# Moving element-wise work to GpSimd and the first weights to the head of the queue

## The chip, the cores and the metric

The kernel runs on one core of one Trainium2 chip. The core has five engines that work side by side, each through its own instructions strictly in their order: TensorE (PE in the rows; PEld is its loading of weights), VectorE (DVE), ScalarE (ACT), GpSimd (POOL) and SyncE (SP, which here issues most of the DMAs). The metric is the device time of the core in microseconds (us), from one launch.

## The reference

The inputs pass three stages. For B = 4 batch items, H = 8 heads, S = 576 rows and D = 64 columns:

```
a     = softmax(causal(q k^T / sqrt(D)))                 # scores
local = a v
q_p   = phi(q) = max(q, 0) + exp(min(q, 0))              # elu(q) + 1
mem   = (q_p M_prev) / (q_p . z_prev + 1e-6)
attn  = g mem + (1 - g) local,  g = sigmoid(beta) by head
x = attn as 2304 rows x 512
x = (s * relu(x w_in)^2 + b) w_out        # 512 -> 2048 -> 512
x = h * tanh(softplus(h)) w_out2, h = x w_in2             # mish, 512 -> 2048 -> 512
```

The weights of both feed-forward layers arrive as 64-bit floats.

## The kernel before

**Attention.** 64 zero rows are put ahead of the queries, so that 640 rows make five row tiles of 128, t = 0 to 4. The unit of work is a *pair*: two heads of one batch item, for one group of row tiles. Group TA is the tiles 0 to 2, group TB the tiles 3 and 4; 16 of each make 32 pairs, here numbered 0 to 31 in the order in which they are worked on. Pairs 0 to 3 are the TA pairs of the first batch item; from pair 4 on TB pairs (even numbers) and TA pairs (odd numbers) take turns. For each pair and head a tile `Pt` of 128 rows has 64 columns for the memory part in front, and behind them the scores of row tile t, 64 + 128 t columns. The steps, with the lines of the profile:

1. L494 (GpSimd) min(q, 0) for the whole pair, 384 columns for TA and 256 for TB; L495 (ScalarE) its exponential; L496, L497, L498 (VectorE) phi(q), times z, and the row sums; L492 and L500 gate and reciprocal of these, `nm`.
2. L526 (TensorE) scores into PSUM; L532 (VectorE) adds the mask, takes the row minimum and copies into `Pt`; L543 (GpSimd) writes the memory part; L540 (ScalarE) the exponential with row sums `rs`.
3. L561 (VectorE) reciprocal of the gated `rs`; L558 scales the scores of each row tile by it, in place, one instruction for each tile and head. Which engine does it is in the string `E_NORM`, by t: GpSimd for t = 0, 1, 2 and VectorE for t = 3, 4.
4. L581 (TensorE) turns `Pt` by blocks of 128, in two groups for a head of a TA pair and three for one of a TB pair; L586 copies each group from PSUM to `PT`. `E_TURN` says on which engine, by head and group: all on ScalarE but the first group of the second head of TA pairs (384 columns), which is VectorE's.
5. L603 (TensorE) the product with [M; v]; L617 (ScalarE) copies it out. For pairs 0 to 3 L614 and L615 make the first 256 rows of layer 1's input from it at once.

**Weights.** Each of the 32 pieces (128 x 512) of layer 1's weights, four for each of eight weight tiles (`w_in` and `w_out`, r = 0 to 3), is made from 64-bit words by `convert`: an SP load of 512 KB (L653); the high words times 2^-112 (L660, 512 elements, every second 4-byte word, on ScalarE by `C_W`); the low words (L665, ScalarE); sign and merge (L667, L669, VectorE); a rounded high part (L676, ScalarE) and the rest (L679, VectorE). Layer 2's pieces do the same by `C2_W`, into another place.

**Layer 1** (L762 in, L838 out, with L811, L817, L820, L822 between) works on blocks of 256 rows, later 512. Its first matmul needs the outputs of pairs 0 to 3 and the first weights. Layer 2 (L968, L1034) follows.

**What sets the order.** Nothing is issued as it is written. `Plan` collects steps with an engine, a duration (`act_us`, `dve_us`, `pool_us` or a number in the call), a priority and what they wait for, runs a list scheduler over them, and writes the program in the order found. Attention pairs have priority 7 x their number, layer 1's matmuls 500 and more, so that TensorE takes attention work first and fills what is left with layer 1. Before the first matmul of layer 1 it fills idle time with products of zeros (L1215). A number in a call thus moves instructions on every engine.

Of the kernel before, what the change touches and what calls it, by code (L numbers as in the profile page):

```python
# [9 lines left out]
F32 = mybir.dt.float32  # L10
# [5 lines left out]
ALU = mybir.AluOpType  # L16
# [7 lines left out]
PE, ACT, DVE, POOL, DMA = range(5)  # L24
# [8 lines left out]

E_NORM = 'PPPDD'
E_TURN = {0: 'AAAAA', 1: 'DAAAA'}
C_HI, C_W, C2_W = 'AAAA', 'AAAA', 'AAAA'
C_LO = 'DDDD'
# [16 lines left out]
def pool_us(n):  # L54
    return 0.2 + 0.0033 * n

# [5 lines left out]
def on(letter):  # L62
    return {"A": ACT, "D": DVE, "P": POOL}[letter]
# [266 lines left out]
def attention_then_two_ffn(ctx: ExitStack, tc: tile.TileContext, qk, qz, vm, beta,  # L330
# [3 lines left out]
    nc = tc.nc  # L334
# [97 lines left out]
    def pair(b, p, prio, g, place=None, apart=False):  # L432
# [4 lines left out]
        def add(engine, us, f, r=(), w=(), keep=(), share=1.0):  # L437
            attention_steps.append(plan.add(engine, us, prio, f, r, w, keep=keep, share=share))
# [30 lines left out]
        def q_rows():  # L469
            return part(qn_b, 1, n_t + 1)[:, :, 1:]  # L470
# [22 lines left out]

        add(POOL, 0.3 + 0.0032 * n_e, lambda: nc.gpsimd.tensor_scalar_min(ex.t, q_rows(), 0.0), [qn_b], [ex])  # L494
        add(ACT, act_us(n_e), lambda: nc.scalar.activation(ex.t, ex.t, AF.Exp), [ex], [ex])  # L495
# [66 lines left out]
        for t in g:  # L562
            for i in range(2):
                e = on(E_NORM[t])
                n = D + P * t
                us = act_us(n) if e == ACT else 0.05 + dve_us(n, True) if e == DVE else pool_us(n)
                add(e, us, lambda i=i, t=t, e=e: scale(i, t, e), [done, Pt_in[i, t]], [Pt_in[i, t]], [Pt[i, t][0], rs])
# [71 lines left out]
    def convert(layer, prio, which, r, j, raw, after=()):  # L639
# [7 lines left out]
        def words():  # L647
            return raw.t[:, :1024].rearrange("p (n two) -> p n two", two=2)

        def f32():  # L650
            return w.t.bitcast(F32)
# [6 lines left out]
        e = on((C_W if layer == 1 else C2_W)[j])  # L658
        add(e, 0.52 if e == ACT else 0.335, prio,
            (lambda: nc.scalar.activation(f32(), words()[:, :, 1].bitcast(F32), AF.Copy, scale=2.0 ** -112)) if e == ACT else  # L660
            (lambda: nc.vector.tensor_scalar(f32(), words()[:, :, 1].bitcast(F32), 2.0 ** -112, None, op0=ALU.mult)),
            [raw], [w])
# [438 lines left out]
    for i, p in enumerate(pieces):  # L1101
        convert(1, 3.0 * i if i < 8 else 28.0 + 3.0 * (i - 8), *p, raws[i])
    conversion_left = add(NONE, 0.0, 0.0, lambda: None, after=plan.steps[n:])
# [160 lines left out]
```

## Time and profile before

| | us |
|---|---|
| median of 3 runs | 996.66 (992.43 to 996.84) |
| profiled execution | 996.01 |
| its span, first to last instruction | 994.2 |
| TensorE busy | 972.1 (98%) |
| VectorE busy | 680.9 (68%) |
| ScalarE busy | 635.5 (64%) |
| GpSimd busy | 183.2 (18%) |

The page divides the span in 40 slices of 24.9 us. TensorE's digit is 9 in nearly all of them, but these shares are means over stages with different limits: in the first twelve slices, but for the very first, VectorE and ScalarE stand at 7 to 9 too and GpSimd at 3 to 8. The last output of attention (L617) is copied near 338 us, in slice 14; from then on GpSimd does no arithmetic, and VectorE and ScalarE reach 9 in single slices alone. So the stretches are read one by one, by windows.

### The profile page before, as it was taken

The numbers are of one execution on the slowest core, as the hardware profiler recorded it, in microseconds if no ns is written. First come the engines' busy times: TensorE is split into PE (matmuls) and PEld (weight loads), VectorE is DVE, ScalarE is ACT, GpSimd is POOL, SyncE is SP. The second block draws the span as 40 slices with busy tenths as digits, with TensorE's granted clock in tenths as the row PEclk, the third lists the DMA queues.
The fourth block names the chain that finished last, engine by engine and source line by source line (L and its number), as shares of the span: only waits on it lengthen the run. The fifth ranks groups of instructions, "written<-read, shape, count | busy, mean of one in ns | idle before, by whom it ended". The sixth has DMA issues, their size and how long they took to land.

```text
span 994.2 us, 18129 instructions
## 1 busy us (share of the span) xinstructions
PE 972.1 (98%) x6342; PEld 854.8 (86%) x6342; DVE 680.9 (68%) x1638; ACT 635.5 (64%) x1361; POOL 183.2 (18%) x346
## 2 busy tenths in 40 slices
PE   6999989999999999999999999999999999999998
PEld 4767767877787898888888888999999999999998
DVE  5989889877775467778412143489965799567864
ACT  5988888777775567899645566366643466434552
POOL 5863443465531000000000000000010001100100
PEclk9999999999999999999999999999999999999999
DMA  9962565654441389997700116288677666676465
GB/s 259 300 185 65 172 198 152 168 135 130 127 129 55 94 264 294 297 324 250 260 3 1 43 64 221 96 294 273 212 268 240 202 209 211 237 248 203 150 221 175
DMA packets 103083, 184.69 MB, mean 186 GB/s; under 512 B 17232, under 2 KB 77648, under 8 KB 95696
## 3 DMA queue, kind: packets, MB, share of 16 engines
q1 hardware_dynamic: 95504, 132.15, 43.0%
q0 software_dynamic: 7056, 51.38, 15.2%
q8 instruction: 50, 0.82, 0.3%
q14 instruction: 41, 0.34, 0.1%
q10 hardware_dynamic: 432, 0.01, 0.0%
HBM read 141.04 MB, written 42.47 MB: 185 GB/s over the span
## 4 chain that ended last, share of the span: by engine, by line
PE 79%; issue 7%; DMA 6%; ACT 4%; POOL 2%; DVE 1%; POOLq 0%; SPq 0%; ACTq 0%
PE bank L762 18%; PE bank L838 17%; PE bank L968 15%; PE bank L1034 13%; PE bank L581 5%; PE bank L526 5%; PE bank L603 5%; POOL Pt L558 2%; DMA wo_split_d<-high 1%; DMA woh<-wo_split_d 1%; ACT Pt L540 1%; DMA wol<-wi_split_d 1%; DMA wih<-in_w_in 1%; ACT stage L660 1%; DMA stage<-in_w_in 1%
## 5 line engine op out<-in xcount | busy, mean ns | idle before, releaser
L1034 PE MATMUL bank<-woh,S 128*128 128x256 f32 x792 | 107.4, 283 | 1.4 <-DMA woh<-wo_split_d 1.4
L540 ACT ACTIVATE Pt<-Pt,mx 128x64 f32<-128x64 f32 (+4 forms) x160 | 89.0, 563 | 22.2 <-DVE mx L532 22.0
L1034 PEld LDWEIGHTS bank<-woh,S 128*128 128x128 f32 x792 | 100.8, 192 | 1.6 <-ACT S L690 1.6
L1034 PE MATMUL bank<-wol,S 128*128 128x256 f32 x720 | 98.1, 283 | 0.0
L968 PE MATMUL bank<-wi,woh 128*128 128x384 f32 x426 | 93.9, 334 | 0.0
L949 POOL DMA_DIRECT2D wol<-wo_split_d x17 | 9.2, 541 | 457.4 <-DVE wi L691 365.6
L1034 PEld LDWEIGHTS bank<-wol,S 128*128 128x128 f32 x720 | 91.8, 192 | 0.0
L586 ACT COPY PT<-bank 128x384 f32<-128x384 f32 (+1 forms) x144 | 62.9, 490 | 31.2 <-PE bank L581 28.7
L543 POOL TENSOR_SCALAR Pt<-ex,nm 128x64 f32<-128x64 f32 x160 | 61.6, 404 | 112.4 <-DVE nm L500 54.1
L581 PE MATMUL bank<-ident,Pt 128*128 128x128 f32 x480 | 73.1, 284 | 9.0 <-POOL Pt L558 6.8
L532 DVE CUSTOM_DVE_ANT_0 Pt<-bank,mask 128x320 f32<-128x320 f32 (+3 forms) x160 | 64.0, 430 | 22.6 <-PE bank L526 21.6
L968 PE MATMUL bank<-wi,wol 128*128 128x384 f32 x294 | 76.0, 335 | 0.4 <-DMA wol<-wi_split_d 0.4
L968 PEld LDWEIGHTS bank<-wi,woh 128*128 128x128 f32 x426 | 75.6, 188 | 0.6
L581 PEld LDWEIGHTS bank<-ident,Pt 128*128 128x128 f32 x480 | 55.7, 145 | 17.5 <-POOL Pt L558 10.4
L558 POOL TENSOR_SCALAR Pt<-Pt,rs 128x64 f32<-128x64 f32 (+2 forms) x96 | 60.5, 650 | 40.0 <-DVE rs L561 33.1
L838 PE MATMUL bank<-xh,woh 128*128 128x512 f32 x240 | 64.2, 389 | 0.0
L821 DVE TENSOR_TENSOR xh<-g,xh 128x512 fp32r<-128x512 f32 x30 | 20.6, 688 | 60.2 <-ACT xh L819 60.2
L968 PEld LDWEIGHTS bank<-wi,wol 128*128 128x128 f32 x294 | 53.0, 188 | 0.9 <-DMA wol<-wi_split_d 0.6
L838 PEld LDWEIGHTS bank<-xh,woh 128*128 128x128 f32 x240 | 45.0, 188 | 9.1
L762 PE MATMUL bank<-yh,wi 128*128 128x512 f32 x192 | 51.4, 391 | 0.4 <-ACT g L811 0.4
L811 ACT ACTIVATE g<-bank 128x512 f32<-128x512 f32 x48 | 28.6, 595 | 33.4 <-PE bank L762 33.4
L762 PEld LDWEIGHTS bank<-yh,wi 128*128 128x128 f32 x192 | 35.3, 188 | 7.6 <-ACT g L811 0.8
(256 smaller groups left out, 2335.2 us busy)
## 6 DMA issues: line engine op xcount, KB each, us to landing
wol<-wo_split_d POOLq DMA_DIRECT2D x17, 1024.0 KB, 5.2
woh<-wo_split_d POOLq DMA_DIRECT2D x16, 1024.0 KB, 5.4
stage<-in_w_out SPq DMA_DIRECT2D x23, 512.0 KB, 5.0
wo_split_d<-high SPq DMA_DIRECT2D x44, 256.0 KB, 4.3
stage<-in_w_in SPq DMA_DIRECT2D x21, 512.0 KB, 5.4
stage<-wi_d SPq DMA_DIRECT2D x24, 384.0 KB, 4.8
wi_split_d<-woh SPq DMA_DIRECT2D x8, 1024.0 KB, 4.9
wol<-wi_split_d POOLq DMA_DIRECT2D x8, 1024.0 KB, 5.1
```

The lines of the kernel that those rows point to most:

```text
L526: nc.tensor.matmul(ps[i].t[:, :hi - lo], qkt(t * P, P)[rows(i)], kt(lo, hi - lo)[rows(i)], start=True, stop=True)
L532: nc.vector.tensor_tensor_reduce(at_t(i, t, D + lo, D + hi), ps[i].t[:, :hi - lo], mask[:, SP - w + lo:SP - w + hi], -SCALE, mx.t[:, i, t: ...
L540: nc.scalar.activation(at_t(i, t, D, w + D), at_t(i, t, D, w + D), AF.Exp, bias=mx.t[:, i, t + k:t + k + 1], scale=-1.0, accum_out=rs.t[:, ...
L543: add(POOL, 0.33, lambda i=i, t=t: nc.gpsimd.tensor_scalar(at_t(i, t, 0, D), ex.t[:, i, t - lo_t, :], nm.t[:, i, t - lo_t:t - lo_t + 1], 1 ...
L558: (nc.vector if e == DVE else nc.gpsimd).tensor_scalar(x, x, r, *((None, ALU.mult) if e == DVE else (1.0, ALU.mult, ALU.mult)))
L581: nc.tensor.transpose(ps.t[:, x, :], at_t(i, t, c * P, (c + 1) * P), ident)
L586: (nc.vector.tensor_copy if dve else nc.scalar.copy)(PT[i].t[:, x:x + n], ps.t[:, :n])
L603: nc.tensor.matmul(pv.t[rows(i), cols].rearrange("p (t q) -> p t q", q=P), vx()[:, i, c, :], PT[i].t[:, f[0]:f[-1] + 1:f[1] - f[0] if len( ...
L762: nc.tensor.matmul(ph, w_at(nm, r, cc)[:, o:o + P], x_at(x, cc), start=(begin and part == 0 and cc == 0), stop=(part == 2 and cc == NCC - ...
L838: nc.tensor.matmul(acc[ec // per].t[:, (ec % per) * n:(ec % per + 1) * n], w_at(nm, fc // FPR, fc % FPR)[:, ec * P:(ec + 1) * P], t(x)[:, ...
L968: nc.tensor.matmul(ps.t[:, :H2], w[i // 4].t[:, j, kk, i % 4], x[kk].t[:, k], start=begin and part == kk == 0, stop=part == 2 and kk == 1, ...
L1034: nc.tensor.matmul(acc[t].t[:, :DH], s.t[:, j, t * P:(t + 1) * P], x.t[:, k, q % 4], start=q == part == 0, stop=q == NQ2 - 1 and part == 2)
```

## The change

```diff
-E_NORM = 'PPPDD'
-E_TURN = {0: 'AAAAA', 1: 'DAAAA'}
-C_HI, C_W, C2_W = 'AAAA', 'AAAA', 'AAAA'
+E_NORM = {True: 'PPP', False: 'PPPPP'}
+E_TURN = {0: 'AAAAA', 1: 'AADAA'}
+C_HI, C_W, C2_W = 'AAAA', 'PPPP', 'AAAA'
...
 def pool_us(n):
-    return 0.2 + 0.0033 * n
+    return 0.3 + 0.0008 * n
...
-        add(POOL, 0.3 + 0.0032 * n_e, lambda: nc.gpsimd.tensor_scalar_min(ex.t, q_rows(), 0.0), [qn_b], [ex])
+        add(POOL, 0.25 + 0.0009 * n_e, lambda: nc.gpsimd.tensor_scalar(ex.t, q_rows(), 0.0, 1.0, op0=ALU.min, op1=ALU.mult), [qn_b], [ex])
...
-                e = on(E_NORM[t])
+                e = on(E_NORM[b == 0 and lo_t == 0][t])
...
-        add(e, 0.52 if e == ACT else 0.335, prio,
+        add(e, 0.52 if e == ACT else 0.75, prio,
             (lambda: nc.scalar.activation(f32(), words()[:, :, 1].bitcast(F32), AF.Copy, scale=2.0 ** -112)) if e == ACT else
-            (lambda: nc.vector.tensor_scalar(f32(), words()[:, :, 1].bitcast(F32), 2.0 ** -112, None, op0=ALU.mult)),
+            (lambda: nc.gpsimd.tensor_scalar(f32(), words()[:, :, 1].bitcast(F32), 2.0 ** -112, 1.0, op0=ALU.mult, op1=ALU.mult)),
...
-        convert(1, 3.0 * i if i < 8 else 28.0 + 3.0 * (i - 8), *p, raws[i])
+        convert(1, 3.0 * i - 1.0 if i < 8 else 28.0 + 3.0 * (i - 8), *p, raws[i])
```

So L558 is GpSimd's for every tile (64 instructions of 448 and 576 columns leave VectorE); the high words of layer 1's 32 pieces are GpSimd's too (line 661 there, L661); the minimum carries a second operation, a product with 1; the copy of L586 that VectorE does is now the first group of the second head of TB pairs (512 columns) and no longer that of TA pairs (384); the priority of the first eight pieces is lower by 1, which puts the first of them ahead of pair 0; and the scheduler reckons with shorter GpSimd times.

The new numbers move instructions everywhere. VectorE at the start, from its fifth instruction (`ex`, `nm`, `Pt` belong to pair 0, `stage` and `wi` to the first piece of weights), before:

```order
L496 SCALAR_TENSOR_TENSOR ex_143<-wih_0_128,ex_143 128x384
L497 TENSOR_TENSOR wih_0_128<-ex_143,wih_0_128 128x2x192
L498 TENSOR_REDUCE nm_162<-wih_0_128 128x2x3
L492 SCALAR_TENSOR_TENSOR nm_162<-nm_162,igate 128x2x3
L500 RECIPROCAL nm_162<-nm_162 128x2x3
L532 ISA Pt_0_165,mx_167<-bank_110,mask 128x64
```

and now:

```order
L667 SCALAR_TENSOR_TENSOR stage<-stage 128x512
L669 SCALAR_TENSOR_TENSOR stage<-stage 128x512
L679 TENSOR_TENSOR wi_155<-stage,wi_155 128x512
L496 SCALAR_TENSOR_TENSOR ex_151<-wih_0_130,ex_151 128x384
L497 TENSOR_TENSOR wih_0_130<-ex_151,wih_0_130 128x2x192
L498 TENSOR_REDUCE nm_178<-wih_0_130 128x2x3
```

The whole conversion of the first piece stands ahead of pair 0. On ScalarE L665 and L676 of that piece stand ahead of pair 0's L495 in the same way, and on SP its load ahead of pair 0's five.

VectorE where the last of the four pieces of `w_in`, r = 3, is finished (`wil_0_1734`, later `wil_0_1632`); the four L558 are pair 12's. Before:

```order
L558 TENSOR_SCALAR Pt_0_1680<-Pt_0_1680,rs_1683 128x448
L558 TENSOR_SCALAR Pt_1_1681<-Pt_1_1681,rs_1683 128x448
L558 TENSOR_SCALAR Pt_0_1709<-Pt_0_1709,rs_1683 128x576
L558 TENSOR_SCALAR Pt_1_1710<-Pt_1_1710,rs_1683 128x576
L667 SCALAR_TENSOR_TENSOR stage<-stage 128x512 x2
L669 SCALAR_TENSOR_TENSOR stage<-stage 128x512 x2
L496 SCALAR_TENSOR_TENSOR ex_1895<-qn_1851,ex_1895 128x384
L679 TENSOR_TENSOR wil_0_1734<-stage,wih_0_1719 128x512
```

and now:

```order
L669 SCALAR_TENSOR_TENSOR stage<-stage 128x512
L492 SCALAR_TENSOR_TENSOR nm_1791<-nm_1791,igate 128x2x2
L500 RECIPROCAL nm_1791<-nm_1791 128x2x2
L532 ISA Pt_0_1809,mx_1811<-bank_111,mask 128x448
L532 ISA mx_1811 128x1
L532 ISA Pt_1_1810,mx_1811<-bank_112,mask 128x448
L532 ISA mx_1811 128x1
L679 TENSOR_TENSOR wil_0_1632<-stage,wih_0_1607 128x512
```

It was VectorE's row 390 and is now its row 342; the 20 L558 that stood ahead of it are gone, and the masks (L532) of pair 12 have just begun where they were done.

GpSimd at pairs 4 and 5, before (`rs_735` is pair 5; pair 4's four tiles were VectorE's):

```order
L543 TENSOR_SCALAR Pt_1_808<-ex_628,nm_739 128x64
L494 TENSOR_SCALAR ex_845<-woh_0_656 128x384
L558 TENSOR_SCALAR Pt_0_732<-Pt_0_732,rs_735 128x64
L558 TENSOR_SCALAR Pt_1_733<-Pt_1_733,rs_735 128x64
L558 TENSOR_SCALAR Pt_0_799<-Pt_0_799,rs_735 128x192
L558 TENSOR_SCALAR Pt_1_800<-Pt_1_800,rs_735 128x192
```

and now (`rs_699` is pair 4, `rs_772` pair 5, `stage` a piece of layer 1's weights):

```order
L543 TENSOR_SCALAR Pt_1_805<-ex_626,nm_707 128x64
L661 TENSOR_SCALAR stage<-stage 128x512
L558 TENSOR_SCALAR Pt_0_696<-Pt_0_696,rs_699 128x448
L558 TENSOR_SCALAR Pt_1_697<-Pt_1_697,rs_699 128x448
L558 TENSOR_SCALAR Pt_0_724<-Pt_0_724,rs_699 128x576
L558 TENSOR_SCALAR Pt_1_725<-Pt_1_725,rs_699 128x576
L558 TENSOR_SCALAR Pt_0_769<-Pt_0_769,rs_772 128x64
L558 TENSOR_SCALAR Pt_1_770<-Pt_1_770,rs_772 128x64
L558 TENSOR_SCALAR Pt_0_794<-Pt_0_794,rs_772 128x192
L558 TENSOR_SCALAR Pt_1_795<-Pt_1_795,rs_772 128x192
```

Pair 4's scaling now waits in one queue behind the memory parts of pair 5 and a piece of weights.

## Rows read from the trace of the kernel before

**Rows 1.** Span of the core and mean granted clock of TensorE.

```profile
core 0: 994.2 us, clock 0.995
```

**Rows 2.** Stretch, length; busy PE, PEld, DVE, ACT, POOL (instructions); clock; DMA share, GB/s.

```profile
27.00:53.00 26.00, 23.19 (x159) 17.39 (x157) 25.30 (x75) 23.11 (x65) 22.03 (x31) 1.00 1.05 293
...
62.00:100.00 38.00, 38.00 (x298) 30.13 (x298) 36.09 (x113) 34.45 (x88) 16.55 (x30) 1.00 0.42 118
100.00:120.00 20.00, 19.37 (x150) 15.34 (x148) 17.42 (x56) 17.33 (x44) 9.62 (x18) 1.00 0.60 167
120.00:140.00 20.00, 20.00 (x158) 16.25 (x155) 17.99 (x50) 16.20 (x41) 5.91 (x10) 1.00 0.62 187
140.00:160.00 20.00, 17.06 (x113) 12.20 (x113) 16.59 (x51) 17.32 (x44) 8.12 (x17) 0.91 0.66 203
...
200.00:290.00 90.00, 90.00 (x706) 68.54 (x705) 67.33 (x243) 65.06 (x192) 48.50 (x102) 1.00 0.48 130
```

**Rows 3.** TensorE in order of time: start, duration, instruction; the first of layer 1.

```profile
61.89 0.64 PE L762 MATMUL bank<-xh,wi 128*128 128x256 f32 x4
```

**Rows 4.** TensorE, 140 to 151 us: idle time before an instruction in brackets.

```profile
141.25 0.55 PE L581 MATMUL bank<-ident,Pt 128*128 128x128 f32 x3 [0.19 <-POOL Pt L558]
142.59 1.56 PE L581 MATMUL bank<-ident,Pt 128*128 128x128 f32 x8 [0.80 <-POOL Pt L558]
...
149.38 1.91 PE L581 MATMUL bank<-ident,Pt 128*128 128x128 f32 x9 [1.88 <-DVE Pt L558]
```

**Rows 5.** Chain of waits, 130 to 166 us: start, duration, what.

```profile
138.30 4.76 POOL Pt L558 x5
```

**Rows 6.** VectorE in order of time, 148 to 155 us.

```profile
148.79 1.66 DVE L558 TENSOR_SCALAR Pt<-Pt,rs 128x448 f32<-128x448 f32 x4
154.16 0.69 DVE L679 TENSOR_TENSOR wil<-stage,wih 128x512 fp32r<-128x512 f32 x1 [0.83 <-ACT wih L676]
```

**Rows 7.** Groups on VectorE, 60 to 200 us: busy us, mean ns, idle before.

```profile
L558 DVE TENSOR_SCALAR Pt<-Pt,rs 128x576 f32<-128x576 f32 x14 | 6.6, 510 | 0.0
L558 DVE TENSOR_SCALAR Pt<-Pt,rs 128x448 f32<-128x448 f32 x14 | 6.3, 480 | 0.1
L586 DVE COPY PT<-bank 128x384 f32<-128x384 f32 x6 | 3.3, 547 | 0.7 <-PE bank L581 0.7
```

**Rows 8.** Groups on GpSimd, 200 to 290 us.

```profile
L558 POOL TENSOR_SCALAR Pt<-Pt,rs 128x64 f32<-128x64 f32 x12 | 6.5, 553 | 17.8 <-DVE rs L561 17.8
L558 POOL TENSOR_SCALAR Pt<-Pt,rs 128x320 f32<-128x320 f32 x12 | 6.3, 534 | 0.0
L558 POOL TENSOR_SCALAR Pt<-Pt,rs 128x192 f32<-128x192 f32 x12 | 5.3, 452 | 0.0
```

**Rows 9.** Groups on GpSimd, 60 to 200 us.

```profile
L558 POOL TENSOR_SCALAR Pt<-Pt,rs 128x192 f32<-128x192 f32 x12 | 9.3, 789 | 0.0
L558 POOL TENSOR_SCALAR Pt<-Pt,rs 128x320 f32<-128x320 f32 x12 | 8.6, 728 | 0.0
L494 POOL TENSOR_SCALAR ex<-qn 128x256 f32<-128x256 f32 x5 | 4.5, 901 | 1.1 <-DMA qn<-in_qz 1.1
L494 POOL TENSOR_SCALAR ex<-qn 128x384 f32<-128x384 f32 x3 | 3.5, 1169 | 3.0 <-DMA qn<-in_qz 2.9
```

**Rows 10.** Groups on ScalarE, 60 to 200 us.

```profile
L586 ACT COPY PT<-bank 128x384 f32<-128x384 f32 x32 | 14.7, 483 | 5.1 <-PE bank L581 5.0
L660 ACT ACTIVATE stage<-stage 128x512 f32<-128x512 f32 x17 | 11.6, 681 | 0.2 <-DMA stage<-in_w_out 0.2
L586 ACT COPY PT<-bank 128x512 f32<-128x512 f32 x14 | 7.7, 586 | 2.5 <-DVE Pt L558 1.6 <-PE bank L581 0.6 <-ACT xh L782 0.2
```

**Rows 11.** Start in order of time: VectorE's pair 0, ScalarE's first piece.

```profile
6.15 0.56 DVE L496 SCALAR_TENSOR_TENSOR ex<-wih,ex 128x384 f32<-128x384 f32 x1 [1.23 <-ACT ex L495]
...
9.83 0.67 ACT L660 ACTIVATE stage<-stage 128x512 f32<-128x512 f32 x1 [3.71 <-DMA stage<-in_w_in]
```

## The prediction

> **What bounds the kernel now.** I read the engines by stretch first. From 62 us on, where layer 1 begins [rows 3], TensorE is busy without a break in nearly every stretch: whatever attention leaves free is filled with layer 1's matmuls. Work that leaves another engine is therefore worth nothing by itself from there on; only time in which TensorE stands still can be won. There are two such places. One is the start: until 61.9 us TensorE has only attention and products of zeros, and in 27 to 53 us VectorE is busy 25.3 of 26 us while ScalarE has 23.1 and GpSimd 22.0, so VectorE sets the pace of pairs 0 to 3, on whose outputs layer 1 waits. The other is 140 to 160 us: 113 matmuls against 158 in the 20 us before it, at a mean clock of 0.91, which mixes its two levels of 2.4 and 1.2 GHz and follows idle time of the engine [rows 2, 4]. By count (158 - 113) / 158 x 20 = 5.7 us are lost there; by idle time and clock 2.94 + 0.09 x 20 = 4.7 us. One more place, 100 to 120 us with 150 matmuls, lost 1.0 us by count.
>
> What is late in that place? Then I read who ended the waits and the chain of waits there. TensorE waits for scaled tiles, twice GpSimd's and once, 1.88 us, VectorE's [rows 4]; five of GpSimd's scalings took 4.76 us [rows 5]. VectorE does four scalings of pair 12 in 1.66 us from 148.8 on, and only at 154.2 the last low part of `w_in`, r = 3, which layer 1's next matmuls need [rows 6]. VectorE was busy 36.1 of 38 us in 62 to 100 and 35.4 of 40 in 100 to 140 [rows 2]: it is the engine on which weights and attention meet, and TensorE catches up with it.
>
> **The change part by part.** *Scaling of tiles 3 and 4.* 64 instructions leave VectorE, at 0.480 and 0.510 us [rows 7]: 32 x 0.99 = 32 us in all, and 10 x 0.99 = 9.9 us before the place at 154 us. On GpSimd the trace shows no such width. Where little else disturbs it, 192 columns took 0.452 and 320 took 0.534 us [rows 8], 0.64 ns a column, so 448 and 576 would take 0.62 and 0.70 us; in 60 to 200 us the same instructions took 0.789 and 0.728 us [rows 9], some 0.3 us more, so 0.9 to 1.0 us. I take 0.95 in that stretch, and as its ends 0.62 and 1.1. A TB pair's four scalings thus grow from 2 to 3.8 us, off the engine that sets the pace. If that cover is gone, each TB pair costs the 1.8 us.
>
> The two stretches differ by the weights: 60 to 200 us has the conversions with their two-operand instructions on VectorE, 200 to 290 us has none. The Trainium skill says why ("GPSIMD Engine Reference", Key points): GpSimd shares its SBUF interfaces with VectorE and contends with instructions that read two SBUF operands. The 0.337 us on 192 columns agree with that.
>
> *High words on GpSimd.* ScalarE loses 32 x 0.681 = 21.8 us [rows 10]. On GpSimd this operation, 512 elements at a step of two words, is not in the trace. Its lower end is the line of the two-operand scaling, 0.534 + 192 x 0.00064 = 0.66 us; its upper end the one-operation minimum, 1.169 us for 384 and 0.901 for 256 columns [rows 9], which leads to 1.169 + 128 x 0.0021 = 1.44 us. It is written with two operations like the scaling, so I take the nearer end with the disturbance, 0.95 us. Each waits in GpSimd's queue for its DMA, and behind it stand memory parts (L543), for which ScalarE's L540 waits, and scalings, for which TensorE's L581 waits. ScalarE's own wait for these landings was 0.2 us in 17 [rows 10], so that costs nothing unless GpSimd runs ahead.
>
> *Minimum with two operations.* 16 x 1.169 + 16 x 0.901 = 33 us of GpSimd become, by the line of rows 8, 0.57 and 0.49 us each, 17 us. Whether the second operation does that is not shown: the ends are this and no change. It matters to TensorE only in the chain of pairs 0 to 3.
>
> *Copies swapped.* VectorE loses 16 x 0.547 us (384 columns) and gains 16 of 512, between 0.55 and 0.547 x 512/384 = 0.73 us; ScalarE gains 16 x 0.483 and loses 16 x 0.586 [rows 7, 10]. VectorE +2 us in all, ScalarE -1.6: nothing on the path.
>
> *First piece first.* At the start VectorE does L496 of pair 0 at 6.15 us and ScalarE waits 3.71 us, until 9.83, for the first piece [rows 11]. Now pair 0 waits for that piece: its load is 512 KB at some 290 GB/s [rows 2], 1.8 us, ahead of pair 0's; then VectorE's three conversions of about 0.69 us with ScalarE's between them. I estimate L496 at 9 us, 2.5 to 3 us later. But VectorE was idle there, and these three conversions, 2 us of its work, are done in idle time instead of later. Since it sets the pace in 27 to 53 us, this comes back: +0.5 us for pair 0, -2 us by pair 3. Sum -1.5 us; its ends are +3 (pair 0 late, nothing regained) and -5 (ScalarE's 0.68 us for each of some 8 pieces, 5.4 us, also come off the path).
>
> *The place at 154 us.* The last of those conversions is VectorE's row 342 instead of 390. The 20 scalings are 9.9 us of that; the other 28 rows, mostly masks of pair 12 with their read-outs, some 7 us: 17 us less work ahead of it. TensorE in turn is to use the weights sooner, because fewer of layer 1's matmuls and pair 12's products come ahead: about 9 us of its time, plus the 1.5 us of the start. 17 against 10.5 is 6.5 us better, where 5.7 were missing. That closes the gap with about 1 us to spare, and GpSimd's longer queue takes some of that: I count 4.5 of the 5.7 us. The 1.0 us at 100 to 120 us stays.
>
> Sum, against the profiled execution's own 996.0 us (span 994.2 [rows 1] and 1.8 around it; the median of the runs, 996.7, lies 0.65 above): -1.5 - 4.5 = -6.0, so **990.0 us**. From 340 us on the edits touch no instruction; the order shifts there, which I count as 0 with 2 us to either side.
>
> **The rivals.** *GpSimd sets the pace* (slower). In 62 to 155 us it was busy 16.55 + 9.62 + 5.91 + 3/4 x 8.12 = 38 of 93 us [rows 2]. Added are 20 scalings and about 20 pieces of weights, minus some 4 us for the minimum. At my prices that is 38 + 19 + 19 - 4 = 72 us, at the upper ends 38 + 22 + 29 = 89 us. VectorE, the fullest so far, was idle a tenth of the time, so an engine with 89 us of work in order needs 99: 6 us more than the stretch had, with the gap at 150 us in it. With the start's -1.5 that is 1000.5 us, and with the start's +3 some 1005. It decides from about 84 us of work on. For it: GpSimd's 0.8 us on tiles that take 0.45 undisturbed. Against it: half of its time was free.
>
> A page speaks for this one: the Trainium skill ("GPSIMD Engine Reference", Performance versus the Vector engine) gives GpSimd about 2.6 cycles an element at 1.2 GHz, measured with two inputs, against VectorE's one. An estimate from that page would be 1.0 and 1.2 us for tiles of 448 and 576 and 1.1 us for a piece, 38 + 22 + 22 - 4 = 78 us. The 0.64 ns a column of rows 8 are far from it, and only the one-operation minimum of rows 9, 2.1 ns, is near.
>
> *The wait changes its name* (no change): the weights come in time, but TensorE now waits for GpSimd's scalings, 1.8 us longer for each TB pair, and the stall is the same 5.7 us: 994.5 us. For it: the waits in rows 4 end at scalings. Against it: VectorE, with 17 us less ahead of it there, hands the tiles over earlier by more than 1.8 us.
>
> *The first piece holds pair 0* and nothing comes back: 996 + 3 - 4.5 = 994.5 us. For it: everything of pair 0 stands behind it on three engines; against it: VectorE's idle time there.
>
> *ScalarE was the second pace-setter of the start*: 996 - 5 - 5.7 = 985 us. For it: 23.1 of 26 us; against it: VectorE's 25.3.
>
> **How the numbers follow.** Forecast 0.47, GpSimd sets the pace 0.12, the wait changes its name 0.19, pair 0 held 0.08, ScalarE 0.14. Within 0.5% (5 us, about what a measurement of this kernel can tell from no change) lies what ends above 991.5. Of the forecast, 986 to 994 us by its unknown prices, three quarters are faster: 0.35, with ScalarE's 0.14 that is 0.49. The two rivals without change and the forecast's other quarter make 0.38, and GpSimd's 0.12, with 0.01 of pair 0's, 0.13. The range reaches to 984, ScalarE's case with a little more, and up to 999, where GpSimd's case begins.
>
> **What would show it.** Layer 1's first matmul at 60 to 61 us, not 62 or later. In 140 to 160 us, and in any 20 us of 62 to 300, 150 matmuls or more and a clock of 1.00. VectorE with 3 us and more of idle time in 62 to 100 us, and GpSimd's L558 on 448 and 576 columns at 0.9 to 1.0 us there and 0.6 to 0.7 later; L661 at 0.7 to 1.0; L494 at 0.5 to 0.6. It is wrong if TensorE waits for GpSimd by more than 4 us in 62 to 170, if L661 takes over 1.4 us, or if layer 1 starts after 63 us.

## The result: slower, and the profile after

The changed kernel takes 1008.68 us (median of four runs, 1007.94 to 1009.17) against 995.25 us for the kernel before, run beside it: ratio 1.0132, 95% interval 1.0106 to 1.0159. The forecast was 990.0 us and its range ended at 999. The profiled execution has this span [rows 1]:

```profile
core 0: 1006.7 us, clock 0.992
```

The same stretches as [rows 2] (stretch, length; busy PE, PEld, DVE, ACT, POOL with instructions; clock; DMA share, GB/s):

```profile
27.00:53.00 26.00, 20.82 (x110) 14.59 (x108) 18.26 (x58) 15.18 (x42) 21.80 (x38) 0.74 0.94 254
62.00:100.00 38.00, 36.47 (x271) 26.91 (x270) 34.44 (x98) 30.57 (x84) 31.38 (x47) 1.00 0.32 98
100.00:120.00 20.00, 19.00 (x132) 15.28 (x134) 15.83 (x48) 14.24 (x38) 14.32 (x25) 0.91 0.37 111
120.00:140.00 20.00, 18.68 (x138) 14.54 (x135) 17.91 (x42) 15.01 (x33) 13.66 (x18) 1.00 0.67 210
140.00:160.00 20.00, 19.29 (x149) 14.88 (x149) 14.20 (x46) 14.16 (x39) 14.76 (x24) 1.00 0.59 177
200.00:290.00 90.00, 90.00 (x693) 65.92 (x694) 60.67 (x237) 67.28 (x203) 64.54 (x128) 1.00 0.53 143
```

At the start VectorE fell from 25.3 to 18.3 us of 26 and ScalarE from 23.1 to 15.2, while GpSimd kept its 22. Part of the fall is waiting: in these 26 us VectorE stood idle for the high words, which are GpSimd's now (total us, times, longest), where its waits before were 0.8 us in all:

```profile
DVE stage L669 <- POOL stage L661: 3.9, 3, 2.2
```

Behind it, the stall of 140 to 160 us is gone (149 matmuls in place of 113), but 62 to 100 us has 271 in place of 298 and 100 to 140 us 270 in place of 308: 690 in 62 to 160 us where there were 719. Layer 1's first matmul [rows 3] comes 6.7 us later:

```profile
68.55 1.22 PE L762 MATMUL bank<-xh,wi 128*128 128x256 f32 x8
```

A second landmark closes the account: layer 1's first matmul of 512 columns, on the second part of the rows, at 361.7 us before and 372.7 after. TensorE's busy time up to there (stretch, length, busy PE; clock; DMA), before and then after:

```profile
0.00:361.70 361.70, 345.15 (x2602) 0.99 0.56 159
```

```profile
0.00:372.70 372.70, 348.70 (x2585) 0.98 0.56 160
```

Idle time there went from 16.6 to 24.0 us. So of the span's 12.5 us, 11.0 arise before this landmark, 7.4 of them as idle time and 3.6 as busy time that grew (the mean clock is lower, and the products of zeros are much the same, 24.1 and 23.8 us); 1.5 us come later. Who ended TensorE's waits for scaled tiles in 60 to 200 us, in total us, times and longest, before and then after [rows 4]:

```profile
PE bank L581 <- POOL Pt L558: 1.2, 3, 0.8
```

```profile
PE bank L581 <- POOL Pt L558: 5.4, 8, 2.2
```

GpSimd's prices, 60 to 200 us [rows 9]:

```profile
L661 POOL TENSOR_SCALAR stage<-stage 128x512 f32<-128x512 f32 x18 | 13.2, 736 | 4.6 <-DVE wol L679 2.5 <-DVE stage L667 1.1 <-DVE nm L492 0.8
L558 POOL TENSOR_SCALAR Pt<-Pt,rs 128x576 f32<-128x576 f32 x12 | 11.8, 990 | 0.0
L558 POOL TENSOR_SCALAR Pt<-Pt,rs 128x448 f32<-128x448 f32 x12 | 11.7, 987 | 14.6 <-DVE rs L561 8.0 <-DVE mx L532 4.7 <-DVE nm L492 1.9
L558 POOL TENSOR_SCALAR Pt<-Pt,rs 128x192 f32<-128x192 f32 x14 | 8.3, 601 | 0.0
L494 POOL TENSOR_SCALAR ex<-qn 128x384 f32<-128x384 f32 x5 | 7.5, 1494 | 0.4 <-DMA qn<-in_qz 0.4
L494 POOL TENSOR_SCALAR ex<-qn 128x256 f32<-128x256 f32 x3 | 3.2, 1064 | 0.0
```

and undisturbed, 200 to 290 us [rows 8]:

```profile
L558 POOL TENSOR_SCALAR Pt<-Pt,rs 128x576 f32<-128x576 f32 x12 | 9.5, 801 | 0.0
L558 POOL TENSOR_SCALAR Pt<-Pt,rs 128x448 f32<-128x448 f32 x12 | 7.8, 665 | 10.1 <-DVE rs L561 6.1 <-DVE mx L532 4.1
```

The wide scalings cost what was forecast, the high words less; the minimum in two operations got slower, not faster. GpSimd's idle time stands before tiles of 448 columns, the first of a group: it stands in its queue and waits for VectorE, with pieces of weights behind. Where pair 3 was lost shows GpSimd in order of time, before:

```profile
44.42 2.02 POOL L543 TENSOR_SCALAR Pt<-ex,nm 128x64 f32<-128x64 f32 x3
46.53 1.68 POOL L494 TENSOR_SCALAR ex<-wih 128x384 f32<-128x384 f32 x1
49.30 4.85 POOL L558 TENSOR_SCALAR Pt<-Pt,rs 128x64 f32<-128x64 f32 x6 [1.09 <-ACT xh L614]
```

and after:

```profile
46.48 0.65 POOL L661 TENSOR_SCALAR stage<-stage 128x512 f32<-128x512 f32 x1
47.11 0.66 POOL L661 TENSOR_SCALAR stage<-wih 128x512 f32<-128x512 f32 x1
49.87 0.66 POOL L661 TENSOR_SCALAR stage<-wil 128x512 f32<-128x512 f32 x1 [2.10 <-DVE wol L679]
50.51 2.26 POOL L543 TENSOR_SCALAR Pt<-ex,nm 128x64 f32<-128x64 f32 x6
52.86 1.49 POOL L494 TENSOR_SCALAR ex<-wih 128x384 f32<-128x384 f32 x1
57.27 4.79 POOL L558 TENSOR_SCALAR Pt<-Pt,rs 128x64 f32<-128x64 f32 x6 [2.92 <-ACT ex L495]
```

Three pieces stand ahead of pair 3's memory parts, and one of them waits 2.10 us until VectorE (L679) has read the buffer into which it writes. Another 2.92 us pass before the scaling, until ScalarE (L495) is done. The pair's scaling starts 8.0 us later, its output ends at 67.0 in place of 61.3 us. The low part of [rows 6] comes no earlier than before, 155.09 us in place of 154.16. It stands behind the masks of pair 12 now, and these wait for TensorE's scores:

```profile
153.99 0.62 DVE L532 CUSTOM_DVE_ANT_0 Pt<-bank,mask 128x448 f32<-128x448 f32 x1 [2.17 <-PE bank L526]
155.09 0.69 DVE L679 TENSOR_TENSOR wil<-stage,wih 128x512 fp32r<-128x512 f32 x1
```

TensorE's first products with the low parts of this weight tile stand at the same time, before and then after:

```profile
158.67 1.22 PE L762 MATMUL bank<-xh,wil 128*128 128x256 f32 x8
```

```profile
158.66 1.22 PE L762 MATMUL bank<-xh,wil 128*128 128x256 f32 x8
```

What filled 140 to 160 us in its place is layer 1's output products (L838), left over from the stretches before: 78 of them ran in 62 to 140 us, where 138 had. In 140 to 160 us, L838 alone, before and then after (stretch, length; busy PE, PEld; clock; DMA):

```profile
140.00:160.00 20.00, 0.95 (x8) 0.74 (x7) 0.91 0.66 203
```

```profile
140.00:160.00 20.00, 7.46 (x56) 6.67 (x55) 1.00 0.59 177
```

### The profile page after: what moved, and what is told of

Same layout as the page of the kernel before. It is cut to its first block, busy times and chain, and to the rows that moved or that the text cites. A ratio compares the mean times of both kernels' runs of the same rounds, so it can differ in the third digit from the quotient of the medians.

```text
span 1006.7 us, 18212 instructions
## 1 busy us (share of the span) xinstructions
PE 977.4 (97%) x6333; PEld 856.3 (85%) x6333; DVE 665.9 (66%) x1574; ACT 616.5 (61%) x1329; POOL 259.2 (26%) x442
## 4 chain that ended last, share of the span: by engine, by line
PE 47%; issue 12%; DMA 6%; ACT 2%; POOL 1%; DVE 1%; POOLq 0%; SPq 0%; ACTq 0%; DVEq 0%
PE bank L838 13%; PE bank L762 13%; PE bank L968 12%; PE bank L1034 7%; DMA woh<-wi_split_d 2%; DMA raw<-in_w_out 1%; DMA wol<-wo_split_d 1%; DMA woh<-wo_split_d 1%; DMA wi_d<-sc 1%; PE bank L603 1%; PE bank L581 1%; DMA wo_split_d<-high 1%; POOL woh L949 0%; ACT high L690 0%; POOL wol L949 0%
## 5 line engine op out<-in xcount | busy, mean ns | idle before, releaser
L558 POOL TENSOR_SCALAR Pt<-Pt,rs 128x64 f32<-128x64 f32 (+4 forms) x160 | 107.5, 689 | 74.1 <-DVE rs L561 37.5
L1034 PE MATMUL bank<-wol,S 128*128 128x256 f32 x828 | 111.9, 283 | 0.4 <-DMA wol<-wo_split_d 0.4
L1034 PEld LDWEIGHTS bank<-wol,S 128*128 128x128 f32 x828 | 105.3, 191 | 0.8 <-issue 0.8
L586 ACT COPY PT<-bank 128x384 f32<-128x384 f32 (+2 forms) x144 | 61.3, 472 | 61.5 <-PE bank L581 54.0
L968 PE MATMUL bank<-wi,woh 128*128 128x384 f32 x423 | 97.1, 335 | 0.8 <-DMA woh<-wi_split_d 0.8
L1034 PE MATMUL bank<-woh,S 128*128 128x256 f32 x684 | 93.1, 283 | 0.0
L1034 PEld LDWEIGHTS bank<-woh,S 128*128 128x128 f32 x684 | 87.0, 192 | 0.0
L532 DVE CUSTOM_DVE_ANT_0 Pt<-bank,mask 128x320 f32<-128x320 f32 (+3 forms) x160 | 64.1, 429 | 27.1 <-PE bank L526 25.1
L968 PE MATMUL bank<-wi,wol 128*128 128x384 f32 x297 | 70.2, 334 | 0.0
L838 PE MATMUL bank<-xh,woh 128*128 128x512 f32 x240 | 64.2, 389 | 0.0
L811 ACT ACTIVATE g<-bank 128x512 f32<-128x512 f32 x48 | 28.6, 597 | 53.5 <-PE bank L762 46.7
L838 PEld LDWEIGHTS bank<-xh,woh 128*128 128x128 f32 x240 | 45.0, 188 | 9.1
```

What stands on the lines that cost most here:

```text
L532: nc.vector.tensor_tensor_reduce(at_t(i, t, D + lo, D + hi), ps[i].t[:, :hi - lo], mask[:, SP - w + lo:SP - w + hi], -SCALE, mx.t[:, i, t: ...
L558: (nc.vector if e == DVE else nc.gpsimd).tensor_scalar(x, x, r, *((None, ALU.mult) if e == DVE else (1.0, ALU.mult, ALU.mult)))
L586: (nc.vector.tensor_copy if dve else nc.scalar.copy)(PT[i].t[:, x:x + n], ps.t[:, :n])
L811: add(ACT, act_us(m) - 0.04, ew, lambda: nc.scalar.activation(rt.t, ph.t[:, :m], *((AF.Relu,) if big else (AF.Copy, 0.0, sb[:, 0:1]))), [p ...
L838: nc.tensor.matmul(acc[ec // per].t[:, (ec % per) * n:(ec % per + 1) * n], w_at(nm, fc // FPR, fc % FPR)[:, ec * P:(ec + 1) * P], t(x)[:, ...
L968: nc.tensor.matmul(ps.t[:, :H2], w[i // 4].t[:, j, kk, i % 4], x[kk].t[:, k], start=begin and part == kk == 0, stop=part == 2 and kk == 1, ...
```

## The experiments

The theories: (1) GpSimd's queue became the pace; (2) the first piece ahead of pair 0 holds the start; (3) the numbers by which the scheduler reckons give a bad order, 3a whatever GpSimd takes, 3b only because GpSimd takes longer than they say; (4) any new order is worse. Each kernel is timed against the kernel before, run on the same chip (its medians were 993.5 to 995.4 us). All results in one table: ratio with its 95% interval; layer 1's first matmul and the landmark of 512 columns; TensorE's idle time up to that; GpSimd's busy time in 62 to 155 us.

| kernel | us | ratio | first | landmark | idle | GpSimd |
|---|---|---|---|---|---|---|
| before | 995.25 | 1 | 61.9 | 361.7 | 16.6 | 38.0 |
| changed | 1008.68 | 1.0132 (1.0106-1.0159) | 68.6 | 372.7 | 24.0 | 71.1 |
| A1 minimum in one operation, same order | 1005.8 | 1.0124 (1.0095-1.0153) | 66.9 | 371.0 | 24.2 | 68.0 |
| A2 true number for the minimum | 1002.83 | 1.0102 (1.0069-1.0134) | 66.3 | 373.0 | 23.6 | 73.6 |
| A3 wide scalings on VectorE | 1007.79 | 1.0145 (1.0109-1.0180) | 71.1 | 375.3 | 25.6 | 53.5 |
| A4 high words on ScalarE | 1003.42 | 1.0089 (1.0064-1.0113) | 68.5 | 370.7 | 24.6 | 61.9 |
| A5 first piece behind pair 0 | 1006.19 | 1.0136 (1.0107-1.0164) | 61.6 | 375.6 | 25.7 | 71.4 |
| B1 before, new numbers only | 1004.14 | 1.0103 (1.0078-1.0127) | 56.7 | 370.6 | 24.9 | 39.7 |
| B2 before, high words on GpSimd | 1001.09 | 1.0069 (1.0047-1.0092) | 68.6 | 370.5 | 18.3 | 56.9 |
| B5 before, minimum in two operations | 995.08 | 1.0005 (0.9989-1.0022) | 58.5 | 358.5 | 15.9 | 40.1 |
| C1 changed, old numbers | 1025.56 | 1.0311 (1.0296-1.0326) | 68.5 | 395.0 | 31.5 | 67.5 |
| C2 before, 0.02 us longer | 993.21 | 0.9987 (0.9970-1.0003) | 62.1 | 365.7 | 16.3 | 39.0 |
| C3 before, 3 to 5% shorter | 995.09 | 1.0005 (0.9991-1.0018) | 58.6 | 361.9 | 16.5 | 36.0 |
| C4 changed, measured numbers | 1003.15 | 1.0083 (1.0066-1.0100) | 65.4 | 369.6 | 21.5 | 74.5 |
| C5 before, measured numbers | 993.28 | 0.9985 (0.9964-1.0006) | 61.0 | 362.5 | 17.9 | 41.9 |
| D4 wide scalings on GpSimd, measured numbers | 992.58 | 0.9983 (0.9969-0.9997) | 53.4 | 359.2 | 17.3 | 60.4 |
| D2 = D4 + high words | 1000.49 | 1.0069 (1.0049-1.0089) | 64.3 | 366.8 | 21.5 | 74.4 |
| D1 = D2 + minimum in two operations | 1000.53 | 1.0064 (1.0041-1.0086) | 63.6 | 367.0 | 22.4 | 76.8 |
| E4 changed order, wide scalings cut | 999.58 | 1.0059 (1.0041-1.0076) | 70.7 | 369.1 | 20.3 | 64.7 |
| E3 changed order, all scalings cut | 995.19 | 1.0003 (0.9991-1.0015) | 66.2 | 362.1 | 18.7 | 60.4 |

The last four columns come from one profiled execution of each kernel. Idle time doesn't hold the products of zeros, which fill TensorE's time before layer 1's first matmul.

### One part put back at a time

A1:

```diff
-nc.gpsimd.tensor_scalar(ex.t, q_rows(), 0.0, 1.0, op0=ALU.min, op1=ALU.mult)
+nc.gpsimd.tensor_scalar_min(ex.t, q_rows(), 0.0)
```

> The changed kernel with the minimum in one operation again, and nothing else: every engine's instructions stand in the same order, since the scheduler's number for it is kept. Theory 1 (GpSimd's queue became the pace, above all because the two-operation minimum takes 1.49 and 1.07 us, not the 0.57 and 0.49 of the prediction): L494 falls to 1.17 us on 384 and 0.85 to 0.90 us on 256 columns, 16 x 0.32 + 16 x 0.19 = 8 us less of GpSimd, the first matmul of layer 1 comes some 2 us earlier than 68.6 us, and the time is 1002 to 1005 us against 1008.7. Theory 2 (the first piece ahead of pair 0 holds the start) and theory 3 (the scheduler's wrong numbers made a worse order, whatever the operation costs): 1007 to 1009 us.

A2:

```diff
-        add(POOL, 0.25 + 0.0009 * n_e, ...
+        add(POOL, 0.2 + 0.0034 * n_e, ...
```

> The changed kernel, the two-operation minimum kept, but the scheduler reckons with what it measured: 0.2 + 0.0034 us a column (1.51 us for 384, 1.07 for 256) in place of 0.25 + 0.0009 (0.60 and 0.48). Theory 3 (the order is bad because of that number): 1000 to 1004 us, the first matmul of layer 1 at 65 us or before. Theory 1 (the operation's own time on a full queue): 1006 to 1009. Theory 2 (first piece): 1007 to 1009, layer 1 still after 67 us.

A5:

```diff
-        convert(1, 3.0 * i - 1.0 if i < 8 else ...
+        convert(1, 3.0 * i if i < 8 else ...
```

> The changed kernel with the first eight pieces at their old priority, so that pair 0 goes first again; all else as changed. Theory 2 (first piece ahead of pair 0 costs the start 6.7 us): layer 1's first matmul at 62 to 63 us in place of 68.6, and 1002 to 1003 us. Theory 1: pair 0 comes 2 us earlier but pairs 1 to 3 wait for GpSimd as before, layer 1 at 67 us, 1006 to 1009 us.

A3:

```diff
-E_NORM = {True: 'PPP', False: 'PPPPP'}
+E_NORM = {True: 'PPP', False: 'PPPDD'}
```

> The changed kernel with tiles 3 and 4 scaled by VectorE again; all else as changed. Pairs 0 to 3 have no such tiles, so the start should stay within 1 us of 68.6 us unless the order there shifts. Theory 1 (GpSimd's queue is the pace between 60 and 180 us): GpSimd loses some 32 us, the idle time of TensorE for scaled tiles there goes, some 5 us, but VectorE is loaded again: 1003 to 1006 us. Theory 2 and theory 3: 1008 us or more, as the stall at VectorE's late low part comes back, 1010 to 1014 us.

A4:

```diff
-C_HI, C_W, C2_W = 'AAAA', 'PPPP', 'AAAA'
+C_HI, C_W, C2_W = 'AAAA', 'AAAA', 'AAAA'
```

> The changed kernel with the high words of layer 1's weights on ScalarE again; all else as changed. So far the minimum's operation, its number, the first piece's priority and the scaling of tiles 3 and 4, each put back alone, gave back 5 us at most of 13. Theory 1 (GpSimd's queue is the pace; its 32 conversions of 0.65 to 0.75 us, some 22 us of work, each with a DMA ahead that can hold the queue, are the largest part not yet put back): 996 to 1001 us, first matmul of layer 1 at 63 to 65 us, TensorE's waits for GpSimd's scalings between 60 and 200 us under 2.5 us in place of 5.4. Theory 3 (every new set of numbers gives an order some 10 us worse than the one of before, whatever the work): 1003 to 1009 us.

None heals it, and none is explained by one theory. A1 falls short of theory 1's range: the minimum is worth 0.1% or nothing. A5 is the clearest miss: theory 2 had the start right, since layer 1 again begins at 61.6 us, and the time wrong, since all of it is lost again, much of it in the old place (stretch, length; busy by engine; clock; DMA):

```profile
140.00:160.00 20.00, 16.84 (x110) 10.93 (x108) 14.29 (x46) 15.26 (x42) 15.83 (x23) 0.91 0.68 203
```

So an early start is worth nothing by itself here; and A3, with the start late and the stall back too (105 matmuls in 140 to 160 us), can't be told from the changed kernel. A2 and A4 gain most, with intervals that still touch the changed kernel's, and one of them changes a number alone. A4 missed all of theory 1's marks: the time, the start, and TensorE's waits for GpSimd's scalings, which rose to 7.2 us. Nor are the pieces all that holds pair 3. Without them its scaling starts at 56.10 us, 1.2 us sooner than in the changed kernel, since GpSimd stands idle before its memory parts until VectorE is done:

```profile
49.71 2.95 POOL L543 TENSOR_SCALAR Pt<-ex,nm 128x64 f32<-128x64 f32 x6 [3.64 <-DVE nm L500]
```

### Numbers or work

B1:

```diff
-    return 0.2 + 0.0033 * n
+    return 0.3 + 0.0008 * n
...
-        add(POOL, 0.3 + 0.0032 * n_e, ...
+        add(POOL, 0.25 + 0.0009 * n_e, ...
```

> The kernel before with the same work on every engine; only the two numbers with which the scheduler reckons GpSimd's scalings and minimum are those of the change (0.3 + 0.0008 and 0.25 + 0.0009 us a column in place of 0.2 + 0.0033 and 0.3 + 0.0032). Theory 3 (the order by wrong numbers is the loss): 1003 us or more, against 993.5 to 995 before. Theory 1 (the work on GpSimd is the loss): 990 to 998 us.

With not one operation changed, three quarters of the loss are there: theory 3. Layer 1 starts 5 us earlier than before, and then TensorE waits (60 to 200 us; total us, times, longest):

```profile
PE bank L526 <- DMA qk<-in_qk: 6.5, 1, 6.5
PE bank L762 <- ACT wih L676: 2.9, 1, 2.9
```

The load of those queries was issued at 122.2 us, when TensorE was all but ready for them. Ahead of it in SP's queue stand loads of weights and stores; in 100 to 134 us such loads waited 16.6 us for VectorE (L669) and stores 8.0 us for ScalarE (L617), in the kernel before 8.1 and 3.9 us. A scheduler that thinks GpSimd's part is done sooner places loads, stores and weights for times that don't come true.

C2 and C3 try theory 4 with `0.22 + 0.0033 * n` and `0.2 + 0.0031 * n`, C5 has `0.6 + 0.0006 * n` for scalings and `0.2 + 0.0026 * n_e` for the minimum, all with the work of before.

> The kernel before, with a meaningless difference: the scheduler reckons a scaling on GpSimd 0.02 us longer (0.22 + 0.0033 us a column). Every engine's order changes from its first instructions on, the work does not. Theory 4 (the order of before is one of the better ones, and any other costs several us): 999 to 1004 us. Theory 3 in its narrow form (only numbers that are wrong by much harm): 993 to 997 us.

> The kernel before, with a second small difference of the same kind: 0.2 + 0.0031 us a column for GpSimd's scalings (2 to 6% less). Theory 4: 999 to 1004 us, with stalls at other places than before. Theory 3 in its narrow form: 993 to 997 us.

> The kernel before, its work unchanged, with numbers near the measured ones (scalings 0.6 + 0.0006 us a column: 0.64, 0.72, 0.79 for 64, 192, 320 columns; measured 0.55 to 0.79; minimum 0.2 + 0.0026: 1.20 and 0.87; measured 1.17 and 0.85 to 0.90). Theory 3 (the truer the numbers the better the order): 990 to 995 us, as before or a little better. If the time is above 999 us, it isn't the truth of the numbers that counts but that they are long, as the numbers of before are for the wide tiles.

All three orders are new on every engine, and all three take the time of before: theory 4 falls. C1 and C4 give the changed kernel other numbers: those of before, and `0.6 + 0.0006 * n` with `0.2 + 0.0034 * n_e`.

> The changed kernel, all its work kept (scalings, high words and two-operation minimum on GpSimd, first piece first), but the scheduler reckons GpSimd's scalings and minimum with the two numbers of before (0.2 + 0.0033 and 0.3 + 0.0032 us a column). Theory 3 (the numbers, through the order they give, are 9 to 10 of the 13 us, as the kernel before with the new numbers alone, 1.0103, suggests): 997 to 1001 us. Theory 1 (the work on GpSimd is the loss): 1003 to 1009 us.

> The changed kernel with numbers close to what was measured: scalings 0.6 + 0.0006 us a column (0.87 and 0.95 for 448 and 576 columns; measured 0.99 and 0.99), minimum 0.2 + 0.0034. Theory 3: as good as with the old numbers or better, 995 to 1000 us. Theory 1: 1003 us or more. Theory 4: anything between 996 and 1008 us, unrelated to how true the numbers are.

C4 regains 0.5 of the 1.3%. Theory 3 had asked for most of it or all (995 to 1000 us); the 1003 us are in the range of theory 1, so numbers near the measured ones don't heal the changed kernel. C1 missed every expectation: numbers that reckon a 576-column scaling at 2.1 us, where 0.8 to 1.0 were measured, stretch attention out (pair 31's output ends at 389.5 us, after the change at 340.5). Which numbers are harmless depends on how much work stands under them.

### GpSimd's own time, with the order kept

B5 puts A1's first line into the kernel before, with the old number.

> The kernel before with one part of the change: the minimum in two operations, the scheduler's number and so every engine's order kept. The operation alone: L494 from 1.17 to 1.49 us on 384 columns and from 0.90 to 1.07 on 256, 8 us more of GpSimd. If each of the minima of pairs 0 to 3 stands in their chain, the first matmul of layer 1 comes 1 to 2 us later and the time is 995 to 997 us against 994; if GpSimd had slack, 993 to 995.

E4 and E3 take the changed kernel, with the same instructions in the same order on every engine, and shorten GpSimd's scalings; the columns left out stay unscaled, so GpSimd does less than any full kernel asks. This

```diff
-            x, r = at_t(i, t, D, P * (t + 1)), ...
+            x, r = at_t(i, t, D, D + (64 if t > 2 else P * t + D)), ...
```

is E4, and E3, with A1's edit beside it:

```diff
-            x, r = at_t(i, t, D, P * (t + 1)), ...
+            x, r = at_t(i, t, D, D + 64), ...
```

> The changed kernel, the order of every engine kept, and only the 64 scalings that the change gave to GpSimd (448 and 576 columns) cut to 64 columns each; the other columns stay unscaled. They fall from 0.99 to about 0.5 us. If the new wide scalings held TensorE: the start stays at 68.6 us, the rest gains 8 us or more, 996 to 1001 us. If the queue as a whole did (narrow scalings, minimum, high words): 1003 to 1007 us.

> The order of the changed kernel kept on every engine, with GpSimd's scalings cut to 64 columns each (the other columns of P stay unscaled) and the minimum in one operation: so GpSimd takes 0.45 to 0.65 us for each scaling, near or below what the scheduler reckoned (0.35 to 0.76), and 1.17 and 0.85 us for the minimum (reckoned 0.60 and 0.48). Theory 3b (the order is good for the times that the scheduler believed and bad for the real ones, the loss is the difference between both on GpSimd): 996 to 1002 us, TensorE's waits for L558 in 60 to 200 us under 2 us instead of 5.4. Theory 3a (the order itself is bad, whatever GpSimd takes) and theory 2 (the first piece): 1004 to 1008 us, layer 1's first matmul still after 66 us.

B5: the operation takes 1.49 us there too, and costs nothing where GpSimd has slack. E3: the changed order is as good as the old one once GpSimd takes about what the scheduler believed, and TensorE's waits for its scalings in 60 to 200 us shrink from 5.4 us to

```profile
PE bank L581 <- POOL Pt L558: 1.4, 2, 0.8
```

That is theory 3b, and 3a falls. It also rules out theory 2 as the cause: the first piece is still first and layer 1 starts at 66.2 us. The late start is made up in 140 to 160 us, which has 150 matmuls, and here the weights are early. TensorE's first products with the low parts of that weight tile:

```profile
150.74 1.22 PE L762 MATMUL bank<-xh,wil 128*128 128x256 f32 x8
```

The waits by themselves don't measure the loss: in 60 to 200 us C4 has 0.4 us of them, and D4, the fastest kernel, 4.1. A scaling cut short frees the engine and also disturbs others less: summed over the instructions of 60 to 200 us, E4 saves 12.7 us on GpSimd and 4.4 on VectorE, where L822 takes 0.78 us in place of 0.97 (0.81 in the kernel before). The runs don't part these two. From A1, E4 and E3: the minimum 0.1% (not distinguishable from nothing), the wide scalings 0.7%, the narrow ones with it about 0.6%. The loss isn't in the new instructions alone but in the whole queue.

### The parts, with numbers that fit

D4 is the kernel before with `E_NORM` all GpSimd's, the copies swapped, and C5's numbers; D2 adds the high words, D1 the minimum in two operations (with 0.2 + 0.0034), C4 the first piece's priority.

> The scaling of tiles 3 and 4 on GpSimd and the swapped copies alone: high words on ScalarE, one-operation minimum, first piece at its old place, with numbers near the measured ones. Theory 1 for this part (GpSimd's longer queue holds TensorE): 999 to 1003 us, waits for L558 of 4 us and more in 60 to 200 us. My prediction's step for this part (VectorE relieved, the stall at 140 to 160 us closes): 989 to 993 us. The rival 'the wait changes its name': 994 to 996 us.

> Scaling of tiles 3 and 4 and the high words on GpSimd, the copies swapped, measured numbers, first piece at its old place, and the minimum in one operation (0.2 + 0.0026 us a column). It differs from the 992.6 us kernel only by the high words, and from the 1000.5 us kernel only by the minimum. If the high words are the rest of the loss: 998 to 1001 us. If the two-operation minimum is: 992 to 995 us.

> The changed kernel with measured numbers (1003.2 us) and the first piece back behind pair 0. Theory 2: layer 1's first matmul some 4 us earlier than its 65.4 us, and 998 to 1000 us. Theory 1: the start as late as it was or the time lost later again, 1002 to 1004 us.

The step that moves the time is D4 to D2, 0.9%: the high words on GpSimd, with the order that the scheduler then finds. Alone, in B2, they cost 0.7% already.

> The kernel before with one part of the change: the high words of layer 1's weights on GpSimd (32 x 0.65 to 0.75 us, 22 us of work leave ScalarE for GpSimd). Theory 1: slower, 999 to 1004 us, with waits for GpSimd's scalings between 60 and 200 us of more than 4 us. Theory 3, and the prediction's price (0.2 us of waiting in all): 990 to 997 us if the order happens to be no worse.

B2 has the time of theory 1 but not its waits for the scalings, 1.5 us in place of over 4. The minimum (D2 to D1) does nothing, the first piece's place (D1 to C4) at most 0.2%, within the intervals; D1's time lies between the ranges of both theories. What the high words do shows D2's GpSimd ahead of pair 3's scaling, where D4, without them, starts it at 43.1 us:

```profile
46.92 0.68 POOL L661 TENSOR_SCALAR stage<-stage 128x512 f32<-128x512 f32 x1
47.56 0.67 POOL L661 TENSOR_SCALAR stage<-wih 128x512 f32<-128x512 f32 x1
48.18 1.62 POOL L494 TENSOR_SCALAR ex<-wih 128x384 f32<-128x384 f32 x1
50.85 1.15 POOL L661 TENSOR_SCALAR stage<-wil 128x512 f32<-128x512 f32 x1 [1.05 <-DVE wol L679]
51.98 5.01 POOL L558 TENSOR_SCALAR Pt<-Pt,rs 128x64 f32<-128x64 f32 x6
```

It is the picture of the changed kernel: pieces ahead in the queue, one of them waiting for VectorE. That the queue's work and not the new order makes the 0.9% is argued from it; no run has D2's order with shorter high words. D4's time is the one of the prediction's step, but the stall has only moved: 120 to 160 us has 242 matmuls, before 271, and a start 8.5 us earlier makes up for that. D4 beats both kernels, by little: 0.17%, interval 0.03 to 0.31%, in line with C5, so the numbers may have as much part in it as the scalings.

## Why the prediction was wrong

*The stall of 140 to 160 us* closed, with 149 matmuls, but not by the prediction's step, and the number is luck. The step had the last low part come after 17 us less of VectorE's work, 6.5 us ahead of TensorE's need. It came 0.9 us later than before, behind masks that waited for TensorE, and TensorE used it at the same time as before (158.7 us). TensorE had work there because it was behind: 56 products of L838 that had mostly been done by then in the kernel before. What was won there, 4.6 us (36 matmuls), was lost in 100 to 140 us (38 matmuls). Of the 2.3 us of idle time in that place 1.3 are waits for GpSimd's scalings, and 1.0 is a wait for a mask, before which VectorE had waited 1.35 us for the high words on GpSimd; behind it the clock fell (0.91 in 100 to 120 us). That is close to the rival "the wait changes its name", except that the weights didn't come in time. The step itself isn't impossible: in E3 the low part is used 8 us earlier.

*The start* failed. The step had VectorE as the pace of pairs 0 to 3 and let it regain what pair 0 loses: forecast 60 to 61 us, measured 68.55, so that a term of -1.5 us came out at +6.7. Pair 0 wasn't even late (its output ends at 26.1 us, before at 27.0). VectorE was idle for 7.7 us in 27 to 53 us, half of it in waits for GpSimd's high words, so it no longer set the pace. I had priced these by their length alone and found that a wait "costs nothing unless GpSimd runs ahead". In the first 60 us they waited 6.2 us for their loads and 2.1 us for VectorE, with parts of the pairs behind them in the queue. That GpSimd's queue alone makes the start late isn't shown: layer 1 starts at 68.5 us without the high words on GpSimd (A4), at 61.6 with them (A5), and at 66.2 with GpSimd's part cut (E3).

*The prices.* Wide scalings 0.99 us (taken 0.95), high words 0.74 (0.95), copies of 512 columns on VectorE 0.68 (0.55 to 0.73): inside. The two-operation minimum, 1.49 and 1.06 us, lies outside both ends (0.57 and 0.49, or no change): I had carried the rate of a scaling over to another operation. A1 and B5 show that this error cost nearly nothing. The Trainium skill's 2.6 cycles an element ("GPSIMD Engine Reference", Performance versus the Vector engine), which the page has for two inputs, gave an estimate of 1.0 and 1.2 us for the wide tiles. The 0.99 us for 448 columns beside VectorE's work agree with it; the 0.99 us for 576 columns there and the 0.67 and 0.80 us of the quiet stretch don't.

*GpSimd sets the pace* was the nearest rival, at 0.12 and with 1000.5 to 1005 us, below the 1008.7 measured. Its sum came out, 72 us forecast in 62 to 155 us and 71.1 measured, by terms that cancel: the wide scalings took 15 us (19 forecast), the high words 13 (19), the minimum 2 more (4 less), and the memory parts, which the sum left alone, 6 more. Its condition, "from about 84 us of work on", was what failed: I took the queue for a pipe that is only full when it is full. The table gives no such bound: 57 us of 93 cost 0.7% in B2, 60 nothing in D4 and E3, 74 cost 0.7% in D2. The sign that I had named for waits on GpSimd didn't show: TensorE waited 3.2 us for it in 62 to 170 us, not over 4, and part of the lateness reached it by way of VectorE.

*The term that was missing.* The prediction has no term for the scheduler's shorter GpSimd numbers. It allows for a new order only behind 340 us ("0 with 2 us to either side"), where little was lost, 1.5 us behind the landmark. By B1 they cost 1.0% with no work moved, by C4 against the changed kernel 0.5%. Reckoned and real times could have been compared beforehand: 0.45 us for 192 columns reckoned now [the change], where [rows 9] has 0.789 in the very stretch.

Open stays how the two causes, GpSimd's time and the numbers, share the 1.3%, since they don't add (E3 removes all of it by GpSimd's time, C4 part by the numbers), what holds the start, and why C1 is so slow.

## What to carry to other kernels

An in-order engine that feeds the critical one can hold it up well below full load: at 76% busy in the changed kernel, at 61% in B2, and not at 65% in D4. Its share tells less than whether work that waits for others (a DMA, a buffer) stands ahead of work that others wait for. Where a scheduler orders the program, its durations are part of the change: put in what the trace shows for the stretch with its contention, and test the new numbers without the new work first. And when one stall closes, count the instructions of the neighbouring stretches before counting the gain: it may be filled with work that is late.

## What was unexpected on the hardware

On GpSimd a second operation made the minimum slower, 1.49 against 1.17 us for 384 columns and 1.06 against 0.85 for 256 (the changed kernel against A1, in one order), while a scaling of 448 columns with two multiplications takes 0.67 us in the quiet stretch. B5, from the profile, 60 to 200 us:

```profile
L494 POOL TENSOR_SCALAR ex<-qn 128x384 f32<-128x384 f32 x3 | 4.5, 1494 | 2.7 <-DMA qn<-in_qz 2.6
```

512 elements at a step of two words (L661) cost no more than a scaling of elements in a row: 0.64 to 0.67 us in the first 60 us, against 0.67 us for 448 and 0.80 for 576 in a row in the quiet stretch. And the start of one and the same order differs from execution to execution: B5, with longer minima, began layer 1 at 58.5 us where the profile of before has 61.9, so a few us at the start of a single profile prove little.
